# One PSUM bank per product and another order of operand sums in a two-layer network computed by seven-product matrix multiplication

## The chip, the cores and the metric

The kernel runs on one core of one Trainium2 chip. The metric is the device time of one execution in microseconds; the median of three executions of the kernel before is 1459.99 us (1458.37 to 1468.76).

## The reference, cut to what matters

```python
p_packed = sm_attn(p, k, v)                 # 8 x 8 heads, 576 tokens, 32 packed, 64 wide
x = sm_attn(q, p_packed, p_packed)          # put together: 4608 tokens x 512
h = max(max(x @ w1, x @ w2), x @ w3)        # 768 wide
x = h @ w_out                               # 512 wide
h = x @ w_in                                # 2048 wide    "third layer"
g = maximum(h, 0) + log1p(exp(-abs(h)))     # softplus
out = g @ w_out2                            # 512 wide     "fourth layer"
```

All arrays are 32-bit floats. The change concerns the last three lines alone.

## The kernel before, in words

The attention and the first two layers fill the first 508 us; they leave x in DRAM. What follows works on five blocks of tokens, numbered c = 0 to 4: three "wide" ones of 2 x 512 tokens and two "narrow" ones of 2 x 384 (`WIDE`, line 62). In each block the third layer runs first and the fourth after it.

**Precision.** Each fp32 operand is split into a high part (a ScalarE copy, line 126) and a low part (a VectorE subtraction, line 128), and each product of two tiles takes three matmuls (high x high, high x low, low x high).

**Seven products.** Both layers multiply in the Strassen-Winograd manner: a 2 x 2 partition of each operand, seven products of sums of the parts instead of eight products.

*Third layer* (`layer3`, line 1048, eight steps j per block). A step computes seven products, each a chain of six matmuls into one PSUM bank (`product`, line 1036). ScalarE copies the first product to SBUF (line 1061); VectorE adds the others to it in seven additions (`plus`, line 1059, each with one operand in PSUM and one in the SBUF tile `h`, which has one buffer); ScalarE then applies softplus to four results (line 1080) and writes them into the SBUF tiles `a00`, `a01`, `a10`, `a11` (in the code a11, a12, a21, a22). `bank` (line 1030) hands out the PSUM space: one tile of *two* banks for every *two* products, the first half to the one and the second half to the other; the pool has four such tiles (line 987), that is all eight banks. The framework puts in the waits between instructions that touch the same tile. Below, the product that gets the first half is called the even one, the other the odd one.

*Fourth layer* (`layer4`, line 1119). 28 steps v per block, four for each of seven products in the order P1, P5, P6, P2, P7, P3, P4 (line 65); a step takes twelve matmuls. `split_g(v)` (line 1104) makes the operand of step v in high and low parts, in tiles with three buffers; it is issued three steps ahead. Four products use sums of the parts of g: S1 = a21 + a22 (for P5), S3 = a11 - a21 (for P7), S2 = a22 - S3 (for P6), S4 = a12 - S2 (for P3). Before the change S1 is formed on VectorE inside `split_g` (line 1094), just ahead of the split that needs it; S3 on GpSimd during the first steps of the fourth layer (line 1102), S2 on VectorE after it, S4 on GpSimd in block 0 and on VectorE in the others. Results of products are added up in three chains X, Y, Z, each in a tile of two banks; `after` (line 1183) keeps a sum in SBUF, adds, transposes 32 x 32 blocks on VectorE (line 1150) and stores rows to DRAM through the SP queue (line 1174).

**What else sets the order.** The order of instructions on every engine is written out by hand: the program order is each engine's order (`manual_schedule`, line 1220). The lists `aside` (in the third layer) and `jobs` (after step v of the fourth) hold other work: in block 0 the splitting of both layers' weights (`split_weights`, line 1009), which come by `load_units` (line 995) into a pool of two buffers shared with x, and go back to DRAM in split form; in later blocks these are read back, 1792 KB for each step (`get_weights`, line 1022, a ring of three tiles). Also there: the sums and splits of the next block's x (`load_x2`, `sum_x2`, `split_x2`, four parts, three for a narrow block). All loads and stores of these stages go through the SP queue, in order.

Of the kernel before, what the change touches and what calls it, by code (L numbers as in the profile page):

```python
# [19 lines left out]
def packed_attention_maxout_softplus(  # L20
# [22 lines left out]
    nc = tc.nc  # L43
# [21 lines left out]
    PRODUCTS = ("P1", "P5", "P6", "P2", "P7", "P3", "P4")  # L65
# [710 lines left out]
    def narrow_wo(raw64, j, k):  # L776
# [29 lines left out]
        for o, in0, in1 in (  # L806
            (t[:, 0], a[:, 1], a[:, 0]),
            (t[:, 1], b[:, 1], t[:, 0]),
            (t[:, 2], b[:, 1], a[:, 1]),
            (t[:, 3], b[:, 0], t[:, 1]),  # L810
        ):
            nc.gpsimd.tensor_tensor(out=o, in0=in0, in1=in1, op=ALU.subtract)
        to_store.append((units(j, "P5", "P6"), t[:, 0:2]))
# [173 lines left out]
    psp = ctx.enter_context(tc.tile_pool(name="psp", bufs=4, space=PSUM, reuse_waits="tile"))  # L987
# [42 lines left out]
    def bank():  # L1030
        k = acc["products"] = acc.get("products", -1) + 1
        if k % 2 == 0:
            acc["bank"] = psp.tile([P, 2, CH], F32, tag="ps", name="ps_3")
        return acc["bank"][:, k % 2]

    def product(c, w, wi, xi):
        wide = BLOCKS[c][1]
        out = bank()[:, :wide]
# [9 lines left out]
    def layer3(c, j, aside):  # L1048
# [7 lines left out]
        h = cp.tile([P, 7, CH], F32, tag="h", name="h")[:, :, :wide]  # L1056
# [27 lines left out]
    def row(m, wide, i):  # L1084
        return m[:, i * 2 * CH : i * 2 * CH + 2 * wide].rearrange("p (b t) -> p b t", b=2)

    def sum_g(c, name, u, n=2):

        wide = BLOCKS[c][1]
        us = slice(u, u + n)  # L1090
        a11, a12, a21, a22 = (g[i, k][:, us, :wide] for i in range(2) for k in range(2))
        if name == "S1":
            t = row(mid[c], wide, 1 + u // 2 % 2)
            add(out=t, in0=a21, in1=a22, op=ALU.add)  # L1094
            return t
        out, in0, in1 = {"S3": (a21, a11, a21), "S2": (a11, a22, a21), "S4": (a11, a12, a11)}[name]
        return out, in0, in1

    def difference(c, name, v, engine):
        for u in (2 * v, 2 * v + 1) if engine is nc.gpsimd else (2 * v,):  # L1100
            out, in0, in1 = sum_g(c, name, u, 1 if engine is nc.gpsimd else 2)
            engine.tensor_tensor(out=out, in0=in0, in1=in1, op=ALU.subtract)  # L1102

    def split_g(c, v):
        pos, u = v // NU, 2 * (v % NU)
        wide = BLOCKS[c][1]
        key = {"P1": (0, 0), "P6": (0, 0), "P3": (0, 0), "P2": (0, 1), "P7": (1, 0), "P4": (1, 1)}
        if PRODUCTS[pos] == "P5":
            src = sum_g(c, "S1", u)
        else:  # L1110
            src = g[key[PRODUCTS[pos]]][:, u : u + 2, :wide]
# [7 lines left out]
    def layer4(c, v):  # L1119
# [4 lines left out]
        if first and v % NU == 0:  # L1124
            acc[CHAIN[name]] = psp.tile([P, 2, CH], F32, tag="ps", name="ps_4")
        ps = acc[CHAIN[name]]
        todo = []
        for i in range(2):
            u = 2 * (v % NU) + i
            tile_no, at = divmod(pos * FP + u, 7)  # L1130
            w = pairs[STEP * c + FP + tile_no]
            for b in range(2):
                for wl, x in ((0, ghi), (1, ghi), (0, glo)):
                    todo.append((i, b, u, w[:, wl, at, b], x[:, i], wl == 0 and x is ghi, x is glo))
        if c == NCH - 1 and v == NV - 1:
            todo.sort(key=lambda m: m[1])
        for i, b, u, l, r, head, tail in todo:
            nc.tensor.matmul(  # L1138
                ps[:, b, :wide],
# [4 lines left out]
                skip_group_check=name in ("P6", "P7", "P4", "P3"),  # L1144
            )

    def turn(c, half, h, src, b):

        o = outs[c, half]
        nc.vector.transpose(  # L1150
            out=o[:, :, h, b],
            in_=src[:, b].rearrange("p (r t) -> p r t", t=32),
        )

    def out_tile(c, half):

        tag = ("a01", "a10")[half]
        wide = BLOCKS[c][1]
        t = ap.tile([P, FP, CH], F32, tag=tag, name="o")
# [23 lines left out]
    def after(c, name):  # L1183

        wide = BLOCKS[c][1]
        m1, m5, u2 = (row(mid[c], wide, i) for i in range(3))
        ps = acc[CHAIN[name]][:, :, :wide]
        last = c == NCH - 1

        def result(m, half, h):  # L1190
            add(out=m, in0=m, in1=ps, op=ALU.add)
            for b in range(2):
                turn(c, half, h, m, b)

        if name in ("P1", "P5", "P6"):
            nc.scalar.activation(
                out={"P1": m1, "P5": m5, "P6": u2}[name], in_=ps, func=AF.Copy
            )
        elif name == "P2":
            out_tile(c, 0)  # L1200
            result(m1, 0, 0)
        elif name == "P7":
            out_tile(c, 1)
            result(m5, 1, 1)
            if last:
                store(c, 1, (1,), [nc.sync])
        elif name == "P3":
            result(u2, 0, 1)
            store(c, 0, (0, 1), [nc.sync])
        else:  # L1210
            for b in range(2):
                turn(c, 1, 0, ps, b)
            if last:
                store(c, 1, (0,), [nc.sync, nc.scalar])
            else:
                store(c, 1, (0, 1), [nc.sync])
# [3 lines left out]
    with tc.manual_schedule(engines={E.PE, E.DVE, E.Activation, E.Pool, E.SP}):  # L1220
        for c in range(NCH):
            more = parts[c + 1]
            for j in range(FP):
                aside = {0: [], 1: [], 2: [], 3: []}
                if c == 0:
# [4 lines left out]
                    aside[3].append((load_weights, j + 4))  # L1230
# [91 lines left out]
```

## Time and profile before

| | us |
|---|---|
| median of three executions | 1459.99 |
| the profiled execution, whole | 1461.07 |
| its span, first to last instruction | 1459.3 |
| TensorE busy within the span | 1268.3 |
| VectorE busy | 864.8 |
| ScalarE busy | 526.9 |
| GpSimd busy | 288.1 |

PE is TensorE's matmuls, DVE is VectorE, ACT ScalarE, POOL GpSimd, SPq the queue that issues DMAs. In a row of the trace, out<-in are the names of tiles in the program; the number in brackets at the end of a row is the idle time of the engine just before, and behind the arrow stands what ended it. PEclk is TensorE's granted clock as a share of full speed. Neighbouring matmuls overlap in the trace, so a matmul's price is read from the distance of starts and not from its duration.

### The profile page before, as it was taken

The page shows a single profiled execution, that of the slowest core. Times are in us where ns is not written, and L with a number is a line of the kernel's source. Part 1 is how long each engine was busy: PE and PEld are TensorE (multiplying, and loading weights), DVE is VectorE, ACT ScalarE, POOL GpSimd, SP SyncE. Part 2 cuts the span into 40 slices and gives each one's busy share as a digit, 9 for nine tenths or more (in the row PEclk, how much of TensorE's full clock was granted, in tenths as well). Part 3 has the DMA queues.
Part 4 walks back from the last instruction along what each step waited for, and adds up shares of the span by engine and source line. Part 5 has one row for each costly group of instructions (what it writes and reads, how often), then busy time and mean ns, then how long its engine had stood idle before and what let it go on. Part 6 is the DMA issues. An engine that isn't in the chain of part 4 may idle for free.

```text
span 1459.3 us, 21380 instructions
## 1 busy us (share of the span) xinstructions
PE 1268.3 (87%) x8599; PEld 1059.8 (73%) x8599; DVE 864.8 (59%) x1151; ACT 526.9 (36%) x767; POOL 288.1 (20%) x248
## 2 busy tenths in 40 slices
PE   8999999999999977777787779977789877897788
PEld 6788998898989955555565556755568766796678
DVE  3866665675765754578633459633387444853375
ACT  4734434344343433345312234312244222422242
POOL 2413122242331132035400015000050000400020
PEclk9999999999999999998899999999999999999999
DMA  9967768697672445446494335564345654575454
GB/s 249 282 170 196 184 179 230 168 242 209 195 203 78 163 187 188 169 140 212 147 311 154 117 113 215 166 223 152 105 161 192 234 197 170 186 251 203 175 197 149
DMA packets 117283, 272.25 MB, mean 187 GB/s; under 512 B 14785, under 2 KB 90305, under 8 KB 106945
## 3 DMA queue, kind: packets, MB, share of 16 engines
q1 hardware_dynamic: 111776, 261.26, 56.8%
q10 hardware_dynamic: 5408, 9.64, 1.8%
q8 instruction: 67, 1.10, 0.3%
q14 instruction: 32, 0.25, 0.1%
HBM read 211.09 MB, written 59.77 MB: 186 GB/s over the span
## 4 chain that ended last, share of the span: by engine, by line
PE 66%; DVE 17%; DMA 7%; issue 4%; ACT 4%; SPq 1%; POOL 1%; DVEq 0%; ACTq 0%; POOLq 0%
PE ps L482 23%; PE ps L1045 23%; PE ps L1138 15%; DVE h L1059 8%; DVE glo L128 3%; PE ps_w L460 2%; DVE a L1102 2%; DMA qraw<-in_q_dram 2%; DVE mid L1094 2%; DMA vt<-in_v_dram 2%; DMA xu<-x2d 1%; ACT ghi L126 1%; ACT a L1080 1%; DVE x2lo L128 1%; DVE wc L128 1%
## 5 line engine op out<-in xcount | busy, mean ns | idle before, releaser
L1045 PE MATMUL ps<-x2hi,wc 128*128 128x512 f32 (+1 forms) x1120 | 363.7, 385 | 127.0 <-DVE h L1059 106.2
L1059 DVE TENSOR_TENSOR h<-h,ps 128x512 f32<-128x512 f32 (+1 forms) x280 | 176.7, 634 | 306.7 <-PE ps L1045 305.3
L1045 PEld LDWEIGHTS ps<-x2hi,wc 128*128 128x128 f32 x1120 | 209.1, 189 | 205.6 <-DVE h L1059 151.9
L1138 PE MATMUL ps<-ghi,wc 128*128 128x512 f32 (+1 forms) x1120 | 340.9, 387 | 20.0 <-ACT ghi L126 20.0
L1138 PEld LDWEIGHTS ps<-ghi,wc 128*128 128x128 f32 x1120 | 216.3, 197 | 58.0 <-ACT ghi L126 26.6
L1138 PE MATMUL ps<-glo,wc 128*128 128x512 f32 (+1 forms) x560 | 219.3, 392 | 25.7 <-DVE glo L128 25.5
L1080 ACT ACTIVATE a<-h 128x512 f32<-128x512 f32 (+1 forms) x160 | 89.7, 584 | 370.9 <-DVE h L1059 370.8
L1102 POOL TENSOR_TENSOR a<-a,a 128x512 f32<-128x512 f32 (+1 forms) x48 | 79.7, 1685 | 684.7 <-DVE mid L1094 684.7
L1045 PE MATMUL ps<-x2lo,wc 128*128 128x512 f32 (+1 forms) x560 | 207.8, 371 | 0.0
L128 DVE TENSOR_TENSOR glo<-a,ghi 128x1024 fp32r<-128x1024 f32 (+1 forms) x120 | 143.0, 1204 | 46.7 <-ACT ghi L126 46.2
L126 ACT ACTIVATE ghi<-a 128x1024 fp32r<-128x1024 f32 (+1 forms) x120 | 115.2, 970 | 118.6 <-PE ps L1138 90.4
L1138 PEld LDWEIGHTS ps<-glo,wc 128*128 128x128 f32 x560 | 109.4, 195 | 54.4 <-DVE glo L128 38.8
L482 PE MATMUL ps<-a2hi,pwhi 128*128 128x288 f32 x576 | 127.6, 303 | 0.1
L482 PE MATMUL ps<-a2hi,pwlo 128*128 128x288 f32 x576 | 123.2, 296 | 0.4 <-DVE pwlo L128 0.4
L482 PE MATMUL ps<-a2lo,pwhi 128*128 128x288 f32 x576 | 123.2, 295 | 0.2 <-DVE a2lo L128 0.2
L1045 PEld LDWEIGHTS ps<-x2lo,wc 128*128 128x128 f32 x560 | 105.9, 189 | 10.9
L128 POOL TENSOR_TENSOR hlo<-m,hhi 128x576 fp32r<-128x576 f32 x41 | 59.2, 1443 | 238.8 <-ACT hhi L126 232.9
L482 PEld LDWEIGHTS ps<-a2hi,pwhi 128*128 128x128 f32 x576 | 91.6, 189 | 15.0 <-ACT m L509 5.3
L511 DVE TENSOR_TENSOR m<-ps,m 128x576 f32<-128x576 f32 x96 | 72.4, 754 | 49.0 <-PE ps L482 47.0
L482 PEld LDWEIGHTS ps<-a2hi,pwlo 128*128 128x128 f32 x576 | 92.6, 188 | 0.6 <-DVE pwlo L128 0.6
L482 PEld LDWEIGHTS ps<-a2lo,pwhi 128*128 128x128 f32 x576 | 92.5, 188 | 0.4 <-DVE a2lo L128 0.4
L128 DVE TENSOR_TENSOR pwlo<-ps_w,pwhi 128x1024 fp32r<-128x1024 f32 (+1 forms) x40 | 44.5, 1113 | 78.3 <-ACT pwhi L126 78.3
(106 smaller groups left out, 1563.9 us busy)
## 6 DMA issues: line engine op xcount, KB each, us to landing
wc<-wic SPq DMA_DIRECT2D x32, 1792.0 KB
wc<-woc SPq DMA_DIRECT2D x32, 1792.0 KB
qraw<-in_q_dram SPq DMA_DIRECT2D x112, 140.0 KB
wic<-wc SPq DMA_DIRECT2D x8, 1792.0 KB
woc<-wc SPq DMA_DIRECT2D x8, 1792.0 KB
kraw<-in_k_dram SPq DMA_DIRECT2D x96, 140.0 KB
vt<-in_v_dram SPq DMA_DIRECT2D x8, 1152.0 KB
wraw<-in_moe_w_dram SPq DMA_DIRECT2D x18, 512.0 KB
```

The source lines that it names most:

```text
L126: nc.scalar.activation(out=hi, in_=src, func=AF.Copy)
L128: engine.tensor_tensor(out=lo, in0=src, in1=hi.bitcast(F32), op=ALU.subtract)
L460: nc.tensor.matmul(ps[cols, G, : units * P].rearrange("p (w x) -> p w x", w=units), ppT[n][rows, cols], wsb[rows, 4 * c : 4 * c + units, g ...
L482: nc.tensor.matmul(o, w, xx, start=first, stop=last)
L511: nc.vector.tensor_tensor(out=m, in0=ps[:, :, :HS], in1=ms[n, f], op=ALU.max)
L1045: nc.tensor.matmul(out, l, r, start=(i == 0), stop=(i == len(terms) - 1))
L1059: add(out=h[:, o], in0=h[:, a], in1=ps, op=ALU.add)
L1080: nc.scalar.activation(out=g[half, k][:, j, :wide], in_=h[:, 2 * k + half], func=AF.Softplus)
L1094: add(out=t, in0=a21, in1=a22, op=ALU.add)
L1102: engine.tensor_tensor(out=out, in0=in0, in1=in1, op=ALU.subtract)
L1138: nc.tensor.matmul(ps[:, b, :wide], l, r, start=first and u == 0 and head, stop=u == FP - 1 and tail, skip_group_check=name in ("P6", "P7" ...
```

## The change

Every product of the third layer, and each half of a chain of the fourth, gets a PSUM tile of one bank; the pool has eight of these. The order of the fourth layer's products becomes P1, P2, P6, P5, P7, P3, P4. S3 is formed during the third layer: on GpSimd after each step in blocks 1 to 4; on VectorE, in pairs, within the steps in block 0. S2, S1 and S4 are formed on VectorE after steps 0 to 3, 4 to 7 and 8 to 11, in all blocks; S2 gets room of its own in a larger `mid` tile, S1 = a11 + S2 and S4 = a12 - S2 are formed in place. `sum_x2` moves from GpSimd to VectorE within the fourth layer, and from VectorE to GpSimd within the third; the x parts of blocks 1 to 4 are split at steps 12, 14, 18 and 22 instead of 0, 2, 9 and 17. The matmuls within a step go operand by operand with both banks, instead of bank by bank. Results are added and transposed bank by bank.

```diff
-    PRODUCTS = ("P1", "P5", "P6", "P2", "P7", "P3", "P4")
+    PRODUCTS = ("P1", "P2", "P6", "P5", "P7", "P3", "P4")
...
-    psp = ctx.enter_context(tc.tile_pool(name="psp", bufs=4, space=PSUM, reuse_waits="tile"))
+    psp = ctx.enter_context(tc.tile_pool(name="psp", bufs=8, space=PSUM, reuse_waits="tile"))
...
-    def bank():
-        k = acc["products"] = acc.get("products", -1) + 1
-        if k % 2 == 0:
-            acc["bank"] = psp.tile([P, 2, CH], F32, tag="ps", name="ps_3")
-        return acc["bank"][:, k % 2]
+    def bank(name):
+        return psp.tile([P, CH], F32, tag="ps", name=name)
...
-        h = cp.tile([P, 7, CH], F32, tag="h", name="h")[:, :, :wide]
+        h = cp.tile([P, 10, CH], F32, tag="h", name="h")[:, :, :wide]
...
+    def form(c, name, u, n, engine):
+        us = slice(u, u + n)
+        a11, a12, a21, a22 = (
+            g[i, k][:, us, : BLOCKS[c][1]] for i in range(2) for k in range(2)
+        )
+        s2 = None if name == "S3" else row(c, 1 + u // 2)
+        out, in0, in1, op = {
+            "S3": (a21, a11, a21, ALU.subtract),
+            "S2": (s2, a22, a21, ALU.subtract),
+            "S1": (a11, a11, s2, ALU.add),
+            "S4": (a12, a12, s2, ALU.subtract),
+        }[name]
+        engine.tensor_tensor(out=out, in0=in0, in1=in1, op=op)
...
-            acc[CHAIN[name]] = psp.tile([P, 2, CH], F32, tag="ps", name="ps_4")
+            acc[CHAIN[name]] = [bank("ps_4") for b in range(2)]
...
-            for b in range(2):
-                for wl, x in ((0, ghi), (1, ghi), (0, glo)):
+            for wl, x in ((0, ghi), (1, ghi), (0, glo)):
+                for b in range(2):
...
+                    if j and j % 2 == 0:
+                        aside[1].append((form, c, "S3", j - 2, 2, nc.vector))
...
-                            aside[1].append((sum_x2, c + 1, part))
+                            aside[1].append((sum_x2, c + 1, part, nc.gpsimd))
...
+                if c:
+                    form(c, "S3", j, 1, nc.gpsimd)
...
+                jobs[0].append((form, c, "S3", FP - 2, 2, nc.vector))
...
-                for part in range(more):
-                    v = 3 + 4 * part
+                for part, v in enumerate((7, 12, 16, 21)):
+                    jobs[v - 1].append((sum_x2, c + 1, part))
+                    jobs[v].append((split_x2, c + 1, part))
...
-                for part, v in zip(range(more), (0, 2, 9, 17)):
+                for part, v in zip(range(more), (12, 14, 18, 22)):
...
             for i in range(NU):
-                jobs.setdefault(1 + i, []).append((difference, c, "S3", i, nc.gpsimd))
-                jobs.setdefault(3 + i, []).append((difference, c, "S2", i, nc.vector))
-                jobs.setdefault(11 + i, []).append(
-                    (difference, c, "S4", i, nc.gpsimd if c == 0 else nc.vector)
-                )
+                for name, v in (("S2", 0), ("S1", 4), ("S4", 8)):
+                    jobs[v + i].append((form, c, name, 2 * i, 2, nc.vector))
+            done = {
+                3: [(keep_sum, c, "X", 0)],
+                11: [(keep_sum, c, "X", 1)],
+                13: [(out_tile, c, 0), (result, c, 0, 0, "Z", 0)],
+                15: [(keep_sum, c, "Y", 2)],
+                19: [(out_tile, c, 1), (result, c, 1, 1, "X", 2)],
+                23: [(result, c, 0, 1, "Y", 1), (store, c, 0, (0, 1), [nc.sync])],
+                27: [(result, c, 1, 0, "X")],
+            }
```

## Rows read from the trace of the kernel before

**Rows 1.** The page's first part: busy time of TensorE and the other engines.

```profile
PE 1268.3 (87%) x8599; PEld 1059.8 (73%) x8599; DVE 864.8 (59%) x1151; ACT 526.9 (36%) x767; POOL 288.1 (20%) x248
```

**Rows 2.** Windows: third and fourth layer of blocks 0, 1, 3, 4 in turn.

```profile
core 0: us, PE busy (x) PEld busy (x) DVE busy (x) ACT busy (x) POOL busy (x), PEclk, DMA share, GB/s
508.28:624.26 115.98, 85.11 (x339) 61.19 (x337) 56.20 (x73) 39.98 (x58) 21.31 (x24) 1.00 0.53 195
624.26:743.10 118.84, 92.82 (x337) 69.97 (x336) 85.91 (x64) 47.69 (x51) 51.66 (x32) 0.87 0.54 177
743.10:855.11 112.01, 85.77 (x338) 61.83 (x336) 44.00 (x67) 24.72 (x40) 0.00 (x0) 0.99 0.46 165
855.11:944.47 89.36, 83.87 (x338) 64.45 (x337) 69.29 (x56) 37.80 (x39) 27.33 (x16) 0.96 0.49 167
...
1145.41:1233.89 88.48, 66.22 (x338) 57.27 (x336) 35.88 (x67) 20.25 (x40) 0.00 (x0) 1.00 0.57 207
1233.89:1303.00 69.11, 63.24 (x338) 59.95 (x337) 52.21 (x54) 29.54 (x37) 16.30 (x12) 0.98 0.59 208
1303.00:1390.59 87.59, 66.22 (x338) 57.27 (x337) 32.90 (x59) 20.25 (x40) 0.00 (x0) 1.00 0.53 197
1390.59:1453.71 63.12, 60.01 (x337) 58.00 (x336) 44.25 (x48) 24.72 (x31) 10.78 (x8) 1.00 0.56 193
```

**Rows 3.** The page's groups: matmuls of the third layer, idle time before them.

```profile
L1045 PE MATMUL ps<-x2hi,wc 128*128 128x512 f32 (+1 forms) x1120 | 363.7, 385 | 127.0 <-DVE h L1059 106.2
```

**Rows 4.** Timeline, third layer of block 2: start, duration, instruction.

```profile
958.08 0.50 PE L1045 MATMUL ps<-x2hi,wc 128*128 128x512 f32 x1 [0.78 <-DVE h L1059]
958.42 0.39 PE L1045 MATMUL ps<-x2lo,wc 128*128 128x512 f32 x1
...
959.35 0.62 PE L1045 MATMUL ps<-x2hi,wc 128*128 128x512 f32 x2
...
959.84 0.60 ACT L1061 ACTIVATE h<-ps 128x512 f32<-128x512 f32 x1 [0.62 <-PE ps L1045]
...
961.19 0.69 DVE L1059 TENSOR_TENSOR h<-h,ps 128x512 f32<-128x512 f32 x1 [3.17 <-PE ps L1045]
...
961.93 0.50 PE L1045 MATMUL ps<-x2hi,wc 128*128 128x512 f32 x1 [0.84 <-DVE h L1059]
```

**Rows 5.** Timeline of ScalarE, fourth layer, a wide and a narrow block.

```profile
930.38 1.06 ACT L126 ACTIVATE ghi<-a 128x1024 fp32r<-128x1024 f32 x1 [1.75 <-PE ps L1138]
...
1288.18 0.85 ACT L126 ACTIVATE ghi<-a 128x768 fp32r<-128x768 f32 x1 [1.27 <-PE ps L1138]
```

**Rows 6.** Groups by form, VectorE: count | busy us, mean ns | idle before.

```profile
L128 DVE TENSOR_TENSOR glo<-a,ghi 128x1024 fp32r<-128x1024 f32 x15 | 18.1, 1214 | 7.4 <-ACT ghi L126 7.4
L1150 DVE STREAM_TRANSPOSE o<-mid 128x512 f32<-128x512 f32 x6 | 3.9, 690 | 0.1
...
L884 DVE TENSOR_TENSOR xu<-xu 128x256 f32<-128x256 f32 x8 | 3.0, 421 | 0.1
...
L1102 DVE TENSOR_TENSOR a<-a,a 128x1024 f32<-128x1024 f32 x4 | 8.1, 2024 | 0.0
```

**Rows 7.** Timeline, third layer of block 0: GpSimd beside VectorE.

```profile
527.79 3.79 POOL L884 TENSOR_TENSOR wu<-wu 128x256 f32<-128x256 f32 x4 [7.46 <-DMA wu<-wi]
528.06 1.55 DVE L128 TENSOR_TENSOR wc<-wu,wc 128x1024 fp32r<-128x1024 f32 x1
529.53 0.67 DVE L1059 TENSOR_TENSOR h<-h,ps 128x512 f32<-128x512 f32 x1
```

**Rows 8.** Timeline, fourth layer of block 0: a weight load and its reader.

```profile
674.49 0.43 SPq L998 DMA_DIRECT2D wu<-wof  x1
...
683.96 1.06 ACT L126 ACTIVATE wc<-wu 128x1024 fp32r<-128x1024 f32 x1 [6.01 <-DMA wu<-wof]
```

**Rows 9.** DMA issues, and one window (columns as in rows 2).

```profile
wc<-wic SPq DMA_DIRECT2D x32, 1792.0 KB
...
1300.00:1320.00 20.00, 16.13 (x85) 14.21 (x85) 6.59 (x12) 3.50 (x7) 0.00 (x0) 1.00 0.99 340
```

More of the change, by code (lines that the diff above doesn't have):

```diff
@@ L1028, in get_weights @@
             )
[L1030 to L1034 removed]
+    def bank(name):
+        return psp.tile([P, CH], F32, tag="ps", name=name)
     def product(c, w, wi, xi):
         wide = BLOCKS[c][1]
[L1038 removed]
+        out = bank("ps_3")[:, :wide]
         terms = [
@@ L1143, in layer4 @@
                 stop=u == FP - 1 and tail,
-                skip_group_check=name in ("P6", "P7", "P4", "P3"),
+                skip_group_check=not first,
             )
[L1147 to L1152, printed above, removed]
-        )
     def out_tile(c, half):
-        tag = ("a01", "a10")[half]
         wide = BLOCKS[c][1]
-        t = ap.tile([P, FP, CH], F32, tag=tag, name="o")
+        t = ap.tile([P, FP, CH], F32, tag=("a00", "a10")[half], name="o")
         outs[c, half] = t.rearrange("p j t -> p (j t)")[:, : 4 * wide].rearrange(
@@ L1181, in store, with result, keep_sum @@
             r += count
-    def after(c, name):
+    def result(c, half, h, chain, m=None):
         wide = BLOCKS[c][1]
[L1186 to L1195, printed above, removed]
+        for b in range(2):
+            src = acc[chain][b][:, :wide]
+            if m is not None:
+                kept = row(c, m)[:, b]
+                add(out=kept, in0=kept, in1=src, op=ALU.add)
+                src = kept
+            nc.vector.transpose(
+                out=outs[c, half][:, :, h, b], in_=src.rearrange("p (r t) -> p r t", t=32)
+            )
+    def keep_sum(c, chain, m):
+        for b in range(2):
             nc.scalar.activation(
-                out={"P1": m1, "P5": m5, "P6": u2}[name], in_=ps, func=AF.Copy
+                out=row(c, m)[:, b], in_=acc[chain][b][:, : BLOCKS[c][1]], func=AF.Copy
             )
[L1199 to L1216, printed above, removed]
     E = mybir.EngineType
@@ L1221, in packed_attention_maxout_softplus @@
         for c in range(NCH):
-            more = parts[c + 1]
+            more, last = parts[c + 1], c == NCH - 1
             for j in range(FP):
@@ new lines, in packed_attention_maxout_softplus @@
+            done = {
[7 more added lines that the diff above has]
+            }
+            if last:
+                done[19].append((store, c, 1, (1,), [nc.sync]))
+                done[27].append((store, c, 1, (0,), [nc.sync, nc.scalar]))
+            else:
+                done[27].append((store, c, 1, (0, 1), [nc.sync]))
@@ L1277, in packed_attention_maxout_softplus @@
                     split_g(c, v + 3)
-                if v % NU == NU - 1:
-                    after(c, PRODUCTS[v // NU])
-                for fn, *args in jobs.get(v, ()):
+                for fn, *args in done.get(v, []) + jobs[v]:
                     fn(*args)
```

69 lines of the change are left out of this document (26 added, 43 removed).

## The prediction, made before the changed kernel was run

> **What bounds the kernel now.** I read the busy times first: TensorE is busy 1268 of 1459 us [rows 1], so the question is where it is not, and where its busy time is slower than it need be. Windows cut at the first matmul of each layer of each block answer that [rows 2]. All of the first 508 us lie ahead of the change. Of the rest, a third layer takes 116.0, 112.0, 112.0 (block 2 is like block 1), 88.5 and 87.6 us, a fourth layer 118.8, 89.4, 89, 69.1 and 63.1 us, though both hold 336 matmuls of the same shape. So the third layer loses time everywhere and the fourth mostly in block 0.
>
> The undisturbed price is read in the fourth layer, where ScalarE makes one operand per step and then waits for TensorE to finish a step: 1.06 + 1.75 = 2.81 us for twelve matmuls in a wide block, 0.85 + 1.27 = 2.12 us in a narrow one [rows 5]. So 28 steps cost 78.7 and 59.4 us, and so should a third layer of the same 336 matmuls.
>
> In the third layer the groups show 127.0 us of idle time ahead of matmuls, nearly all ended by VectorE's additions [rows 3]. The timeline shows the pattern [rows 4]: the row at 959.35 holds two matmuls, the last of one product and the first of the next (even) one, which starts without a wait, in a fresh tile, while ScalarE's copy of the one before only begins at 959.84; but the odd product at 961.93 starts 0.05 us after the addition that read the even one's result ended (961.19 + 0.69), after 0.84 us of idling. It writes the other half of the same tile. So in 280 products 140 wait for a read of the other bank of their tile, 127.0/140 = 0.91 us each, and then lose 0.11 us more, as the step behind a restart is 0.34 us (958.08 to 958.42) and not 0.23 (2.81/12).
>
> **The change part by part.** *One bank per product.* Neighbouring products share no tile, so the wait for the reader of the product before goes; what is left is the wait for the reader of the eighth product before. What is late next? VectorE and ScalarE need per step, one behind the other at worst: seven additions of 0.69, the copy of 0.60 [rows 4] and two softplus behind the last addition (0.6 each, an estimate from the copy of the same shape), with hand-over about 6.8 us, against 42 x 2.81/12 = 9.84 us on TensorE; a narrow step has about three quarters of both (an estimate). TensorE stays the bound, 8 x 9.84 = 78.7 and 59.4 us per layer. The price of a wait that stays is bounded by today's 112.0 and 88.5.
>
> *S3 on GpSimd in the third layer, blocks 1 to 4.* One operation a step, nothing else of weight there. It slows VectorE only where that reads SBUF alone: beside GpSimd a split took 1.55 us, the addition with a PSUM operand 0.67 as ever [rows 7]. Cost 0; if the cover were gone, eight operations a block. The same holds for two `sum_x2` there.
>
> *Block 0's third layer.* Beside the seven additions VectorE has two splits of weights (1.2 to 1.55 and about 0.95) and in three of eight steps an S3 of 1.21: 6.8 + 2.5 + 1.2 = 10.5 us at worst in those, 9.3 in the others, around 9.84. The eight banks even this out: 81 us. Ends: 78.7, and 116.0 if nothing is gained.
>
> One rule is weighed here. The Trainium skill, "SBUF — State Buffer", section "Who interferes with whom", says that a VectorE instruction with two SBUF inputs and a GpSimd one that reads SBUF exclude each other for a whole instruction. The rows show 0.34 us lost (1.55 against 1.21), less than one of the four GpSimd operations (3.79/4 = 0.95). By the rule two or three VectorE instructions a step would lose up to 0.95 each, some 1.5 us more in six steps, and the total below would be 9 us higher.
>
> *Fourth layer, blocks 1 to 4.* It loses 10.7, 10, 9.7 and 3.7 us now (89.4 - 78.7 and so on). S1 was formed right ahead of the split that needed it, beside GpSimd, where an operation of VectorE took 2.02 us instead of 1.21 [rows 6]. After the change GpSimd is idle there and S2, S1, S4 come several steps ahead of need. VectorE per step: split 1.21 + sum 1.21 = 2.4 of 2.81 in steps 0 to 11; steps 12 to 14 with two x parts (2 x (1.21 + 0.91, three quarters of it as an estimate)) and one result (1.21 + 2 x 0.69 = 2.6) 3 x 1.21 + 4.2 + 2.6 = 10.4 against 8.4, within the two steps of lead that a split has; later groups are alike. A narrow block has three quarters of all but the x parts: 8.9 against 6.4 in steps 12 to 14, still within the lead of about 3 us. I take 1 us a layer: 79.7 and 60.4. Ends: 78.7, and today's 89.4.
>
> *Fourth layer, block 0: 118.8 us, 40.1 over the 78.7.* Of these about 15 are the lower clock (0.87 [rows 2]: TensorE falls to 1.2 GHz in places after long waits), the rest waits. Two things remain. First, VectorE's work: 28 splits and 13 sums of 1.21, 12 splits of weights (6 x 2.12), 8 of x (4 x 2.12), 16 additions of x (0.42 each, now here instead of on GpSimd), three results (2.6) and the last transposes (1.4) are 49.6 + 12.7 + 8.5 + 6.7 + 7.8 + 1.4 = 87 us, more than the 78.7 of TensorE. Second, the weights: a load is issued when the split of the tile two before is done, takes 9.5 us from issue to its reader (674.49 to 683.96 [rows 8]; a 1792 KB store stands ahead of it in the same queue), and ScalarE reaches that reader three or four steps (8.4 or 11.2 us) later, minus some 3 us that the last split took. Where it is three it stands about 6 us, with all operands queued behind it. I walked the 28 steps with these prices: TensorE is on time to step 10, loses 1.5 us by step 14, 7.4 at step 15 (a late weight tile, then x's sums and S4 ahead of the operand on VectorE), 4 by step 20, 4.5 at step 22 (the last weight tile) and 3 more: 100 us, and 3 for the clock after the two long waits: 103. Ends: VectorE without any wait, 87 less what stands beside TensorE's tail, so 85; and today's 118.8.
>
> *Bank by bank at the end.* The last block's transposes can start on the first bank while the second is summed: the 5.6 us after the last matmul (1459.3 - 1453.71) become 5.
>
> *SP's queue.* Stores of results now read the tile `a00` instead of `a01`, which the next block's first softplus writes; the store is issued four steps ahead of the block's end: no cost, 2 us a boundary at the outside. Weight loads of 1792 KB per step come every 9.84 or 7.4 us instead of 13.4 or 11. A window with 340 GB/s was reached [rows 9], 5.4 us per load: hidden, with the rival below as the other end.
>
> *Sum.* Start 508.3; block 0: 81 + 103; blocks 1 and 2: 2 x (78.7 + 79.7); blocks 3 and 4: 59.4 + 60.4 and 59.4 + 59.4; end 5: 508.3 + 184 + 316.8 + 238.6 + 5 = 1252.7 us of span. The profiled execution took 1.8 us more than its span (1461.07 against 1459.3) and stood 1.1 us above the median of the runs shown: 1252.7 + 1.8 - 1.1 = **1253 us**.
>
> **The rivals.** *A: transfers become the bound.* A narrow block moves 16 x 1.835 MB of weights and about 3.1 MB of x and results (768 tokens x 512 x 4 bytes each way): 32.5 MB, today in 157.6 us at 207 GB/s, then in 119 us at 273. If no more than 250 is sustained between stores of small rows, it takes 130 us: 11 us more for each of two narrow blocks, and the wide ones (33.6 MB in 158 us, 212 GB/s) hold. With block 0's fourth layer, which has the densest stores, back at 118.8: 1253 + 22 + 16 = 1291. For it: the queue is full (0.99) at a block's beginning. Against: in that window 340 GB/s flowed.
>
> *B: the wait stays.* If the reads hold up the odd product for another reason than the shared tile, the third layers keep 516.1 us instead of 357.2 and only the fourth layers gain: 1253 + 159 = 1412. Against: even products never wait.
>
> *C: slower.* If the wait is tied to the product just before whatever its bank, and the even one is spared today only because its tile is one whose readers are long done, then with a tile for each product all 280 are tied to it: 140 more waits of 0.91 + 0.11 us on top of B, 1412 + 143 = 1555. From about 47 additional waits on (48 us gained in the fourth layers / 1.02) the kernel is slower than before. Against: the even product at 959.35 ran while its neighbour's bank was still unread [rows 4]. The Trainium skill, "PSUM — Partial Sum Buffer", section "PSUM bank collisions raise a hardware error", has engines excluded from each other only within a bank; the trace agrees as far as that row goes.
>
> *D: better.* Block 0's loads come sooner, as the tighter order issues them sooner: its fourth layer at 85, its third at 79: 1233.
>
> **How the numbers follow.** The forecast 0.70, A 0.12, D 0.08, B 0.06, C 0.04. Range: from D's 1233 to A's 1291, opened to 1230 and 1292, which leaves out B and C. A measurement of this kernel tells about 1% (14.6 us) from no change; all cases but C are faster by more: faster 0.95, within 1% 0.01, slower 0.04.
>
> **What would show it.** Right: idle time ahead of line 1045's matmuls falls from 127 to under 15 us; third layers of 79 and 59 us; GpSimd all but idle in the fourth layers; the fourth layer of block 0 the only one with waits of several us, ended by weight loads and VectorE's splits. Wrong: third-layer steps above 10.5 us in blocks 1 to 4, ended by an addition (C or B) or by a load of weights (A).

## The result, and the profile after

The changed kernel takes 1243.65 us (median of four runs, 1240.78 to 1247.03) beside 1459.18 us for the kernel before on the same chip: a ratio of 0.8512 [0.8469, 0.8555]. The forecast was 1253 us, its range 1230 to 1292. The profiled execution took 1240.78 us with a span of 1239.0 us. In the kernel after, the third layer's matmuls stand in line 1042, its additions in 1056, the copy in 1058 and softplus in 1077; the fourth layer's matmuls in 1135, the operand sums in 1099.

The page's first part, against [rows 1]:

```profile
PE 1207.5 (97%) x8599; PEld 1062.0 (86%) x8599; DVE 831.5 (67%) x1182; ACT 526.8 (43%) x782; POOL 213.2 (17%) x224
```

As many matmuls as before now fill 97% of the span instead of 87%. TensorE's own busy time fell as well, by 61 us. Windows cut at the first matmul of each layer, third and fourth layer of blocks 0, 1, 3 and 4 in turn, with the columns of [rows 2]:

```profile
506.62:582.82 76.20, 76.20 (x338) 63.09 (x337) 55.29 (x74) 38.72 (x57) 20.25 (x24) 1.00 0.76 275
582.82:687.39 104.57, 87.47 (x337) 65.82 (x336) 82.15 (x92) 48.27 (x55) 0.00 (x0) 0.92 0.63 211
687.39:764.31 76.92, 76.45 (x338) 62.98 (x336) 38.40 (x57) 24.11 (x39) 14.68 (x15) 1.00 0.71 249
764.31:843.02 78.71, 78.71 (x337) 63.28 (x336) 66.16 (x71) 38.68 (x43) 1.29 (x1) 1.00 0.56 190
...
997.89:1056.16 58.27, 58.27 (x337) 58.26 (x336) 30.67 (x56) 19.75 (x39) 12.74 (x15) 1.00 0.85 315
1056.16:1115.52 59.36, 59.36 (x337) 59.36 (x337) 50.21 (x65) 30.07 (x41) 1.02 (x1) 1.00 0.69 242
1115.52:1174.31 58.79, 58.73 (x337) 58.15 (x337) 30.51 (x56) 19.74 (x39) 7.09 (x7) 1.00 0.79 293
1174.31:1233.83 59.52, 59.52 (x337) 59.20 (x336) 43.25 (x55) 25.38 (x35) 1.02 (x1) 1.00 0.60 205
```

In seven of the ten stages (block 2, not shown, has 76.16 and 78.71) length and PE busy are the same number: TensorE never stands still. In the third layers of blocks 1 and 4 it stands still for 0.47 and 0.06 us. The one stage with real gaps is block 0's fourth layer: 104.57 us long, 87.47 busy, at a granted clock of 0.92. The five third layers together fell from 516.2 to 346.3 us, the five fourth layers from 429.2 to 380.9.

The page's groups of matmuls, against [rows 3] (the number ahead of the arrow is the idle time):

```profile
L1042 PE MATMUL ps<-x2hi,wc 128*128 128x512 f32 (+1 forms) x1120 | 322.2, 367 | 0.5 <-DMA wc<-wic 0.5
L1135 PE MATMUL ps<-ghi,wc 128*128 128x512 f32 (+1 forms) x1120 | 287.7, 378 | 9.1 <-ACT ghi L126 9.0
```

The 127.0 us ahead of the third layer's matmuls became 0.5, and that rest belongs to a load, not to an addition. Timeline of the third layer of block 1, PE and DVE, against [rows 4]:

```profile
854.35 0.62 PE L1042 MATMUL ps<-x2hi,wc 128*128 128x512 f32 x2
854.81 0.39 PE L1042 MATMUL ps<-x2lo,wc 128*128 128x512 f32 x1
855.03 0.62 PE L1042 MATMUL ps<-x2hi,wc 128*128 128x512 f32 x2
...
855.61 0.69 DVE L1056 TENSOR_TENSOR h<-h,ps 128x512 f32<-128x512 f32 x1 [2.18 <-ACT h L1058]
```

Three matmuls take 855.03 - 854.35 = 0.68 us, 0.227 each, straight through the additions on VectorE; a step of 42 takes 9.52 us (76.20/8). What is left shows in the list of waits (who waited <- for whom: us in total, times, longest):

```profile
ACT wc L126 <- DMA wu<-wof: 30.0, 4, 10.0
DVE wc L128 <- ACT wc L126: 17.8, 4, 7.6
...
PE ps L1135 <- ACT ghi L126: 9.0, 2, 4.7
...
PE ps L1135 <- DVE glo L128: 7.9, 6, 2.0
```

All four rows belong to block 0's fourth layer. ScalarE stands 30.0 us for four late weight tiles; VectorE then stands for ScalarE; TensorE stands 17 us for the operands queued behind both.

### The profile page after: what moved, and what is told of

Read it like the earlier page. It is cut to its first block, busy times and chain, and to the rows that moved or that the text cites. A ratio compares the mean times of both kernels' runs of the same rounds, so it can differ in the third digit from the quotient of the medians.

```text
span 1239.0 us, 21402 instructions
## 1 busy us (share of the span) xinstructions
PE 1207.5 (97%) x8599; PEld 1062.0 (86%) x8599; DVE 831.5 (67%) x1182; ACT 526.8 (43%) x782; POOL 213.2 (17%) x224
## 4 chain that ended last, share of the span: by engine, by line
PE 87%; DMA 5%; DVE 4%; issue 2%; ACT 1%; SPq 1%; DVEq 0%; ACTq 0%
PE ps L482 31%; PE ps L1042 27%; PE ps L1135 24%; PE ps_w L460 2%; DMA wu<-wof 2%; PE ps_s L287 1%; DVE glo L128 1%; DMA wc<-wic 1%; DMA wraw<-in_moe_w_dram 1%; PE ps_v L358 1%; PE ps_e L331 1%; DMA xu<-x2d 1%; DVE wc L128 0%; DVE x2lo L128 0%; DMA praw<-in_p_dram 0%
## 5 line engine op out<-in xcount | busy, mean ns | idle before, releaser
L1042 PE MATMUL ps<-x2hi,wc 128*128 128x512 f32 (+1 forms) x1120 | 322.2, 367 | 0.5 <-DMA wc<-wic 0.5
L1135 PE MATMUL ps<-ghi,wc 128*128 128x512 f32 (+1 forms) x1120 | 287.7, 378 | 9.1 <-ACT ghi L126 9.0
L1056 DVE TENSOR_TENSOR h<-h,ps 128x512 f32<-128x512 f32 (+1 forms) x280 | 173.6, 633 | 155.5 <-PE ps L1042 116.1
L1135 PEld LDWEIGHTS ps<-ghi,wc 128*128 128x128 f32 x1120 | 209.5, 191 | 42.1 <-ACT ghi L126 10.8
L1135 PE MATMUL ps<-glo,wc 128*128 128x512 f32 (+1 forms) x560 | 168.3, 379 | 8.0 <-DVE glo L128 7.9
L128 DVE TENSOR_TENSOR glo<-a,ghi 128x1024 fp32r<-128x1024 f32 (+1 forms) x120 | 132.0, 1110 | 33.8 <-ACT ghi L126 33.2
L1099 POOL TENSOR_TENSOR a<-a,a 128x512 f32<-128x512 f32 (+1 forms) x32 | 36.8, 1151 | 567.3 <-ACT a L1077 567.3
L1135 PEld LDWEIGHTS ps<-glo,wc 128*128 128x128 f32 x560 | 104.4, 190 | 27.5 <-DVE glo L128 12.7
```

Source lines behind the costliest of these rows:

```text
L128: engine.tensor_tensor(out=lo, in0=src, in1=hi.bitcast(F32), op=ALU.subtract)
L1042: nc.tensor.matmul(out, l, r, start=(i == 0), stop=(i == len(terms) - 1))
L1056: add(out=h[:, o], in0=h[:, a], in1=ps, op=ALU.add)
L1099: engine.tensor_tensor(out=out, in0=in0, in1=in1, op=op)
L1135: nc.tensor.matmul(ps[b][:, :wide], l, r, start=first and u == 0 and head, stop=u == FP - 1 and tail, skip_group_check=not first,)
```

## The experiments

Twelve runs were made, ten edited kernels and two repeats, in three groups that each shared the runs of the kernel before (1463.25, 1461.80 and 1463.32 us).

### Which part gives what

**E1, the banks alone.** The kernel before, with only its PSUM tiles changed (and, as these ask for it, the fourth layer's results copied and added bank by bank); sums, product order and jobs stay as before.

```diff
-    psp = ctx.enter_context(tc.tile_pool(name="psp", bufs=4, space=PSUM, reuse_waits="tile"))
+    psp = ctx.enter_context(tc.tile_pool(name="psp", bufs=8, space=PSUM, reuse_waits="tile"))
...
+    def bank(name):
+        return psp.tile([P, CH], F32, tag="ps", name=name)
...
-            acc[CHAIN[name]] = psp.tile([P, 2, CH], F32, tag="ps", name="ps_4")
+            acc[CHAIN[name]] = [bank("ps_4") for b in range(2)]
```

> The kernel before with one change: every product and each half of a chain gets a tile of one bank, eight tiles; sums, their order and their engines as before. Theory (an odd product waited for the reader of the other half of its tile): the third layers fall from 516 to about 346 us, as in the changed kernel; the fourth layers stay near their 429 us; time 1285 to 1305 us. Rival 1 (the waits went because S3 and the x sums moved, not because of the banks): third layers stay near 516 us, time 1440 to 1460. Rival 2 (the two parts need each other): fourth layers grow by tens of us as sums come later against a faster TensorE, time above 1330.

Measured: 1296.13 us (1292.7 to 1302.58), ratio 0.8862 [0.8823, 0.8901]. Its third layers take 76.20, 76.18, 76.17, 58.27 and 59.40 us, so the banks alone are the whole gain there. Its fourth layers take 434.9 us together, 5.7 more than before. The window of E1's fourth layer of block 0, and its two largest waits of matmuls:

```profile
581.57:701.69 120.12, 92.13 (x338) 68.58 (x336) 88.73 (x71) 48.36 (x55) 50.62 (x32) 0.89 0.56 188
```

```profile
PE ps L1135 <- DVE glo L128: 28.2, 28, 6.9
...
PE ps L1135 <- ACT ghi L126: 22.1, 16, 2.8
```

GpSimd works 50.62 us in that stage, and over the five blocks TensorE waits for operands 44 times: the fourth layer as it was.

**E2, everything but the banks.** The kernel after, with a tile of two banks for two neighbouring products again, and one of two banks for each chain.

```diff
-    psp = ctx.enter_context(tc.tile_pool(name="psp", bufs=8, space=PSUM, reuse_waits="tile"))
+    psp = ctx.enter_context(tc.tile_pool(name="psp", bufs=4, space=PSUM, reuse_waits="tile"))
...
+    def bank():
+        k = acc["products"] = acc.get("products", -1) + 1
+        if k % 2 == 0:
+            acc["bank"] = psp.tile([P, 2, CH], F32, tag="ps", name="ps_3")
+        return acc["bank"][:, k % 2]
```

> The changed kernel with tiles of two banks again, two products to a tile, as before; order of products and sums as changed. Theory: third layers back at about 516 us, with 0.9 us of idle time ahead of 140 odd products; fourth layers keep 105 + 2 x 79 + 59 + 60 = 381 us; time 1405 to 1420. Rival (the sums pay only beside the banks): fourth layers at 429 us again, time about 1455.

Measured: 1411.35 us (1410.59 to 1412.22), ratio 0.9646 [0.9612, 0.968]. Third layers 513.5 us together, fourth layers 380.0. Windows of E2, third and fourth layer of block 1, and its waits:

```profile
729.65:840.10 110.45, 84.85 (x337) 61.03 (x336) 41.22 (x59) 24.73 (x40) 14.59 (x15) 1.00 0.49 173
840.10:920.14 80.04, 80.04 (x337) 64.28 (x336) 64.13 (x67) 38.28 (x42) 1.28 (x1) 0.98 0.55 187
```

```profile
PE ps L1045 <- DVE h L1059: 104.6, 120, 3.9
...
PE ps L1045 <- ACT h L1061: 20.8, 20, 1.2
```

120 + 20 = 140 waits: one for each odd product, as in the kernel before. E1 gains 167.1 us, E2 51.9; together 219.0, and the full change gained 1461.80 - 1242.92 = 218.9 in the second group of runs. The two parts add up: neither needs the other.

**E4, two banks per tile, but not of neighbours.** E2, with products k and k + 4 in one tile; its pool of four tiles is the same.

```diff
-        if k % 2 == 0:
-            acc["bank"] = psp.tile([P, 2, CH], F32, tag="ps", name="ps_3")
-        return acc["bank"][:, k % 2]
+        if k % 8 < 4:
+            acc["bank", k % 4] = psp.tile([P, 2, CH], F32, tag="ps", name="ps_3")
+        return acc["bank", k % 4][:, k // 4 % 2]
```

> As the second kernel, with tiles of two banks, but products k and k+4 share a tile instead of neighbours. Theory (the wait is for the reader of the other half, which here is long done): third layers 346 us, 1240 to 1255 us. Rival (a tile of two banks costs a wait whoever shares it): third layers near 516 us, 1405 to 1420.

Measured: 1241.1 us in a single execution, as fast as the full change; third layers 76.2, 77.1, 76.2, 58.3 and 58.4 us. The group of its third-layer matmuls:

```profile
L1045 PE MATMUL ps<-x2hi,wc 128*128 128x512 f32 (+1 forms) x1120 | 322.1, 367 | 0.4 <-DMA wc<-wic 0.4
```

So neither the size of a tile nor the number of tiles made the wait, but which two products share one. A matmul that starts a bank waits for readers of the tile's other bank, whose addition is due just then for the neighbour and long done for the product four before. The framework's wait goes by the tile. (The Trainium skill, "PSUM — Partial Sum Buffer", section "PSUM bank collisions raise a hardware error", keeps engines apart by bank. The trace agrees: the wait in E2 went beyond that, and in E1 and the kernel after, where the neighbour's bank is a tile of its own, matmuls run on while it is read, with 0.5 us of idle time in the rows of the kernel after.)

**E3, how many banks it takes.** The kernel after, with two of the eight banks for the third layer and six for the fourth.

```diff
-        return psp.tile([P, CH], F32, tag="ps", name=name)
+        return psp.tile([P, CH], F32, tag=name, name=name, bufs=2 if name == "ps_3" else 6)
```

> The changed kernel with only two one-bank tiles for the third layer's products (the other six for the fourth layer's chains). Theory (it is the sharing with the neighbour that cost, not the number of banks): a product waits for the reader of the product two before, which ends 0.75 us after that one, while the next takes 1.36 us; no wait in most places, some in block 0 where splits stand between the additions: 1241 to 1265 us. Rival (TensorE needs the run ahead of eight banks): one wait per product or step comes back, third layers 80 to 160 us longer in sum, 1320 to 1400.

Measured: 1298.86 us (1294.71 to 1302.23), ratio 0.8874 [0.884, 0.8908]. That is a miss: third layers 400.9 us, 55 more than with eight banks. Its wait, and the timeline at one of these waits:

```profile
PE ps L1042 <- DVE h L1056: 31.3, 40, 1.5
```

```profile
886.58 1.41 DVE L1056 TENSOR_TENSOR h<-h,ps 128x512 f32<-128x512 f32 x2 [0.67 <-PE ps L1042]
...
887.32 0.50 PE L1042 MATMUL ps<-x2hi,wc 128*128 128x512 f32 x1 [0.78 <-DVE h L1056]
```

40 waits in 40 steps: one per step, at its sixth product; a middle step of a wide block takes 10.79 us instead of 9.52. The fourth product is read by two additions that lie apart in the program. The row at 886.58 holds the addition of the fifth product (0.7 us) and then the second reading of the fourth; the sixth product starts at 887.32, when the first of these is over and the second still runs. The fourth product holds one bank for all that time, and one bank alone is left for its successors. The expected 1241 to 1265 us left out how long one result is held.

**E8, two banks and the fourth product copied out.** E3, with a ScalarE copy of that product to SBUF, which both additions then read.

```diff
-        ps = product(c, w, 3, 3)
+        ps = h[:, 7]
+        nc.scalar.activation(out=ps, in_=product(c, w, 3, 3), func=AF.Copy)
```

> The kernel with two banks for the third layer; the fourth product of a step, which two additions read, is first copied to SBUF by ScalarE, so its bank is free at once. If the one wait per step came from that product holding a bank until the fifth one's addition: third layers from 401 back to 346 to 355 us, time 1240 to 1255. If two banks are too few anyway: 1285 to 1300.

Measured: 1265.44 us in a single execution, between the two theories; third layers 369.0 us. Its waits:

```profile
PE ps L1042 <- DVE h L1056: 6.2, 10, 1.1
```

In blocks 1 to 4 a middle step falls from 10.79 to 9.71 us (wide) and from 8.57 to 7.63 us (narrow): the long hold was the cause of most of it there. Block 0's steps stay at 9.7 to 11.4 us, with the splits of weights between the additions, and the first two steps of a block wait up to 3 us more. That rest was not taken apart. Eight banks cover all of it.

### The fourth layer in blocks 1 to 4

**E10, sums just ahead of need.** The kernel after, with S2 and S1 of blocks 1 to 4 formed inside `split_g`, just ahead of the split that needs them. S4 stays early.

```diff
+        if c and name in ("P6", "P5"):
+            form(c, {"P6": "S2", "P5": "S1"}[name], 2 * i, 2, nc.vector)
...
-                    jobs[v + i].append((form, c, name, 2 * i, 2, nc.vector))
+                    if c == 0 or name == "S4":
+                        jobs[v + i].append((form, c, name, 2 * i, 2, nc.vector))
```

> The changed kernel with S2 and S1 of blocks 1 to 4 formed on VectorE right ahead of the split that needs them, as S1 was before the change, but with GpSimd idle and the new order of products. If the lead of several steps is what the sums' 48 us came from: VectorE forms (1.2), waits for the copy (1.06), subtracts (1.2), 3.5 us a step against 2.81 in eight steps, 2 to 6 us a block after the lead of the splits is used up: 1251 to 1267. If it was the crowding (x parts and GpSimd in the same steps): no more than 1 us a block, 1241 to 1247.

Measured: 1273.29 us (1272.9 to 1273.6), ratio 0.8711 [0.8689, 0.8732]. The fourth layers of blocks 1 to 4 take 86.6, 86.6, 67.4 and 65.5 us: of the 34.1 us that the full change gained in these four layers (310.4 to 276.3) 29.8 are gone, with no operation added and GpSimd all but idle (1.3 us a layer). Timeline of E10, VectorE and ScalarE, in block 1, first two steps with S2, then two with S1:

```profile
784.69 1.23 DVE L128 TENSOR_TENSOR glo<-mid,ghi 128x1024 fp32r<-128x1024 f32 x1 [1.21 <-ACT ghi L126]
...
788.26 1.23 DVE L128 TENSOR_TENSOR glo<-mid,ghi 128x1024 fp32r<-128x1024 f32 x1 [1.21 <-ACT ghi L126]
...
801.24 2.35 DVE L1099 TENSOR_TENSOR a<-a,mid 128x1024 f32<-128x1024 f32 x2
...
803.71 1.06 ACT L126 ACTIVATE ghi<-a 128x1024 fp32r<-128x1024 f32 x1 [3.64 <-DVE a L1099]
...
804.80 1.23 DVE L128 TENSOR_TENSOR glo<-a,ghi 128x1024 fp32r<-128x1024 f32 x1 [1.20 <-ACT ghi L126]
...
805.94 2.35 DVE L1099 TENSOR_TENSOR a<-a,mid 128x1024 f32<-128x1024 f32 x2
```

A ring has closed: two sums (2.35), ScalarE's copy (1.06), its subtraction on VectorE (1.23), next two sums: 805.94 - 801.24 = 4.70 us per step, where TensorE needs 2.81. It is so for the operands of steps 12 to 14, where S4 and S1 meet in VectorE's queue, and TensorE takes 4.70 us for each of these steps. Where S2 stands alone ahead of its split the ring takes 788.26 - 784.69 = 3.57 us, and TensorE still keeps 2.81 in steps 8 to 10, as the splits are three steps ahead; but each such step uses up 0.76 us of that lead. So a late sum has a price, hidden at first, and a second sum in the same queue makes it larger. The expectation had the ring of one sum (3.5 us) and the lead; it did not count S4 in the same queue, and so came out at 1251 to 1267 us. In the kernel after, TensorE has no idle time in these layers (78.71 us long, 78.71 busy).

What the run does not show is that the lead alone would be enough: the change also emptied GpSimd and moved the x parts, and E10 keeps both.

**E7, S3 later in the program.** The eight parts of S3 of blocks 1 to 4 stand behind the third layer in the program, not within it.

```diff
-                if c:
-                    form(c, "S3", j, 1, nc.gpsimd)
...
+            if c:
+                for j in range(FP):
+                    form(c, "S3", j, 1, nc.gpsimd)
```

> The changed kernel with S3 in blocks 1 to 4 formed on GpSimd at the beginning of the fourth layer instead of during the third. Theory (the gain of the sums lies in forming them steps ahead of need, by the new order of products, and the third layer as the place is worth little): the S2 sums follow S3 at 3.5 us apiece on GpSimd, are done near step 6 and are needed at step 8; 0 to 3 us a block: 1243 to 1256. Rival (the place of S3 carries most of the 48 us that the sums were worth): 8 to 12 us a block, 1272 to 1292.

Measured: 1243.66 us (1242.35 to 1245.65), ratio 0.8507 [0.8492, 0.8523]: as the full change. But the edit did not move the work. Windows of E7, third and fourth layer of block 1 (GpSimd is POOL, the fifth pair of numbers):

```profile
691.50:768.42 76.92, 76.45 (x337) 62.98 (x336) 38.29 (x57) 24.08 (x39) 14.64 (x15) 1.00 0.70 249
768.42:847.14 78.72, 78.72 (x338) 63.28 (x336) 66.14 (x71) 38.68 (x43) 1.30 (x1) 1.00 0.54 188
```

GpSimd works 14.64 us in the third layer and 1.30 in the fourth; in the kernel after it is 14.68 and 1.29. GpSimd's queue has no other work left at that point, so each part of S3 starts when softplus has written its operands, wherever its line stands. E7 is in effect the full change once more: what the place of S3 is worth was not tested.

### The fourth layer of block 0

The full change ran again in the group of the next kernels. 

> The changed kernel once more, as the measure for the three beside it: 1240 to 1247 us.

Measured: 1242.92 us (1242.75 to 1244.75), ratio 0.8506 [0.8491, 0.8521]; block 0's fourth layer 104.4 us.

**E5, the load ahead of the store.** The store of a split weight tile, with which `split_weights` ended, becomes a job of its own behind the load of the next tile.

```diff
-            nc.sync.dma_start(
-                out=(wic[s] if s < FP else woc[s - FP]),
-                in_=t.rearrange("p h a k x -> p (h a k x)").bitcast(F32),
-            )
...
+    def store_weights(s):
+        nc.sync.dma_start(
+            out=(wic[s] if s < FP else woc[s - FP]),
+            in_=pairs[s].rearrange("p h a k x -> p (h a k x)").bitcast(F32),
+        )
...
+                    aside[3].append((store_weights, j + 2))
+                    jobs[v + 1].append((store_weights, FP + t + 2))
```

> The changed kernel with one exchange in block 0: the load of the next weight tile is issued ahead of the store of the one just split, not behind it. Theory (in block 0's fourth layer ScalarE stands still because each load of 896 KB queues behind a store of 1792 KB): the 9.5 us from issue to reader become about 5, ScalarE's waits for these loads fall from 30 us to 10 to 15, the layer from 104.6 to 92 to 97 us; time 1230 to 1237. Rival (VectorE's 87 us of work set that layer, or the loads are slow by themselves): 102 to 105 us, time 1239 to 1247.

Measured: 1231.98 us (1229.04 to 1233.2), ratio 0.8423 [0.8407, 0.844]. SP's issues and ScalarE's reader of the same tile, in the kernel after, with the window from the load's issue to its reader:

```profile
623.06 0.33 SPq L1017 DMA_DIRECT2D woc<-wc  x1
623.43 0.43 SPq L998 DMA_DIRECT2D wu<-wof  x1
...
632.54 1.06 ACT L126 ACTIVATE wc<-wu 128x1024 fp32r<-128x1024 f32 x1 [9.37 <-DMA wu<-wof]
```

```profile
623.43:632.54 9.11, 6.81 (x28) 4.84 (x27) 4.14 (x4) 0.00 (x1) 0.00 (x0) 1.00 0.87 302
```

And in E5, with the same window, that of the whole layer, and its wait:

```profile
623.35 0.36 SPq L998 DMA_DIRECT2D wu<-wof  x1
623.75 0.56 SPq L1019 DMA_DIRECT2D woc<-wc  x1
...
629.70 1.06 ACT L126 ACTIVATE wc<-wu 128x1024 fp32r<-128x1024 f32 x1 [6.86 <-DMA wu<-wof]
```

```profile
623.35:629.70 6.35, 6.29 (x27) 4.79 (x26) 4.51 (x4) 0.00 (x1) 0.00 (x0) 1.00 0.71 228
584.52:678.79 94.27, 83.81 (x338) 63.16 (x336) 82.03 (x92) 48.34 (x55) 0.00 (x0) 0.98 0.68 236
```

```profile
ACT wc L126 <- DMA wu<-wof: 15.0, 4, 6.9
```

From issue to reader it is 6.4 us (629.70 - 623.35) instead of 9.1 (632.54 - 623.43), and ScalarE was there before the tile both times. In the kernel after the DMA engines are busy for 0.87 of that stretch, and at 302 GB/s 2.75 MB pass in it: the store (1.84 MB) and the load (0.92 MB) together. The four loads with a wait took 10.0, 9.1, 9.4 and 10.4 us, and in E5 6.7, 6.4, 6.0 and 5.9. The four waits halve to 15.0 us, the layer shrinks by 10.3, and the granted clock rises from 0.92 to 0.98 with the shorter waits, which is part of that (PE busy 87.47 to 83.81). This kernel is faster than the kernel before and than the full change (1242.75 to 1244.75 us in the same group).

**E5 again**, in the third group of runs. 

> The kernel with the load ahead of the store once more, beside the next ones: 1229 to 1234 us.

Measured: 1233.15 us (1229.89 to 1241.01), ratio 0.844 [0.8413, 0.8467]; the layer takes 94.3 us.

**E6, less work for VectorE.** The kernel after, with block 0's sums of x in the fourth layer on GpSimd, as before the change.

```diff
-                    jobs[v - 1].append((sum_x2, c + 1, part))
+                    jobs[v - 1].append((sum_x2, c + 1, part, nc.gpsimd))
```

> The changed kernel with block 0's four sums of x in the fourth layer on GpSimd, as before the change. If VectorE's amount of work sets that layer, 6.7 us less of it give 97 to 99 us there and 1234 to 1238. If the late weight loads set it, the layer stays within 3 us of 104.6 (VectorE's operations beside GpSimd take up to 2.0 us instead of 1.2, which takes back what the move gives): 1240 to 1250.

Measured: 1244.63 us (1243.79 to 1249.47), ratio 0.852 [0.85, 0.8539]; the layer takes 106.4 us. VectorE is busy for 81.83 us of it, against 82.15 in the kernel after: the move hardly relieved it, for the reason that E9 shows. So this run does not tell whether relief for VectorE would help.

**E9, both edits.** E5 and E6 together.

> Load ahead of the store, and block 0's sums of x on GpSimd in the fourth layer. If with the loads early VectorE's amount of work is the bound, 6.7 us less of it bring the layer from 94.3 to 88 to 90 us: 1225 to 1229. If the operations that VectorE runs beside GpSimd take back what the move gives, as without the exchange: 94 to 97 us, 1231 to 1236.

Measured: 1235.73 us (1231.97 to 1236.65), ratio 0.8449 [0.8428, 0.8469]; the layer takes 94.7 us. The groups by form, in that layer alone, first of E5:

```profile
L128 DVE TENSOR_TENSOR glo<-a,ghi 128x1024 fp32r<-128x1024 f32 x24 | 28.7, 1213 | 2.2 <-ACT ghi L126 2.2
...
L884 DVE TENSOR_TENSOR xu<-xu 128x256 f32<-128x256 f32 x16 | 6.1, 420 | 2.2 <-DMA xu<-x2d 2.0
```

and of E9:

```profile
L128 DVE TENSOR_TENSOR glo<-a,ghi 128x1024 fp32r<-128x1024 f32 x24 | 30.3, 1283 | 2.2 <-ACT ghi L126 2.2
...
L884 POOL TENSOR_TENSOR xu<-xu 128x256 f32<-128x256 f32 x16 | 24.2, 1534 | 88.5 <-DVE glo L128 52.4 <-DMA xu<-x2d 35.8
```

The sixteen sums cost VectorE 6.1 us (16 x 0.42 = 6.7 without overlap) and GpSimd 24.2; beside them VectorE's other operations get longer (24 splits by 1.6 us), so that its busy time falls by 82.03 - 80.85 = 1.2 us only. Most of GpSimd's time is waiting, as the first of its sums in E9 shows, with ScalarE's reader:

```profile
610.35 5.97 POOL L884 TENSOR_TENSOR xu<-xu 128x256 f32<-128x256 f32 x1 [52.42 <-DVE glo L128]
...
616.36 1.06 ACT L126 ACTIVATE x2hi<-xu 128x1024 fp32r<-128x1024 f32 x1 [5.93 <-POOL xu L884]
```

The shortest of the sixteen takes 0.74 us; this one lasts as long as five VectorE operations on SBUF tiles that follow each other without a gap (610.23 to 615.73). ScalarE waits for the slow sums, 16.9 us in this layer against 7.2 for VectorE's in E5. What keeps this layer at 94 and not at 78.7 us was not separated further: VectorE is busy 82 of the 94, and neither E6 nor E9 took enough work from it to tell.

## Why the prediction was right

**The mechanism held.** The shared tile made the odd product wait (E2, E4), the banks removed it with nothing in its place (E1), and in blocks 1 to 4 the sums set ahead of need gave most of the rest (E10). Rival B was priced at 1412 us as the case in which only the fourth layers gain; E2, which is that case, took 1411.35. Rival C fell with E1 and E4: no product became tied to the one before it. Of D the faster third layer of block 0 came, the faster fourth did not.

**By its steps**, in us of span (first numbers predicted, then found): start 508.3, 506.6; block 0 81 and 103, 76.2 and 104.6; blocks 1 and 2 each 78.7 and 79.7, found 76.9 and 78.7, then 76.2 and 78.7; block 3 59.4 and 60.4, 58.3 and 59.4; block 4 59.4 and 59.4, 58.8 and 59.5; end 5, 5.1. The span is 13.7 us shorter than predicted (terms rounded): 10.9 in the third layers, 1.7 at the start, 1.3 in the fourth layers, and the end 0.1 the other way. The start is scatter: it lies between 505.4 and 510.7 us in the runs here. Against the median it is 9.4, as the profiled run lies 2.9 us below that and had been taken 1.1 above.

**The term that was mis-sized is the third layer's pace.** It was taken over from the fourth, 2.81/12 = 0.234 us for a matmul, 9.84 for a step. Found were 0.227 and 9.52 (narrow: 7.28 for 7.42). The trace before held that pace too. Matmuls of block 2's third layer, beside those of [rows 4]:

```profile
960.03 0.61 PE L1045 MATMUL ps<-x2hi,wc 128*128 128x512 f32 x2
...
960.71 0.39 PE L1045 MATMUL ps<-x2hi,wc 128*128 128x512 f32 x1
```

From 959.35 to 960.03 and on to 960.71 three matmuls take 0.68 us each time, 0.227 apiece. Why the same shape runs 3% faster in the one layer than in the other, both at a granted clock of 1.00, stays open. The second size was the wait's: 0.91 + 0.11 us. Block 1 fell from 112.01 to 76.92, which is 1.25 us for each of 28 waits: 26.2 us were idle (112.01 - 85.77), 0.94 each, and 9.3 us lay in TensorE's busy time (85.77 to 76.45). The trace shows where: the last matmul ahead of the stop at 961.93 starts at 960.71 and counts as busy for 0.39 us, though in a running stream it costs 0.227. So 0.16 us of every stop are booked as busy, which the sum left out; 0.11 are the step behind the restart, and the rest of the 1.25 the slightly longer steps after it.

**Block 0's third layer** was given 2.3 us for an uneven load on VectorE. None came: eight banks bridge it, and each step takes 9.5 us. The Trainium skill, "SBUF — State Buffer", section "Who interferes with whom", has a VectorE instruction with two SBUF inputs and a GpSimd one that reads SBUF keep each other out; by that, the sum was to be 9 us higher. GpSimd's additions of that layer in the trace after (shortest, median and longest in ns):

```profile
L884 POOL TENSOR_TENSOR wu<-wu x24: 730/739/1517, 508.0 to 555.6; 128x256 f32<-128x256 f32 x24
```

The trace agrees that each waits for the other: three 128x768 splits that found an addition under way took 1.18 to 1.33 us, the others 0.95, and additions that found a split under way took up to 1.52 us instead of 0.74. The prediction had looked at VectorE's side alone. The estimate of 9 us was too large, as one VectorE operation a step met GpSimd, lost 0.38 us at most, and the layer lost nothing.

**Block 0's fourth layer** came out at 104.6 against 103, with long waits where the walk had put them: steps 14 and 15 take 7.26 and 7.63 us, steps 21 and 22 take 7.69 and 5.29 (walked: 15 and 22). That the total fits so well is in part luck. The walked losses add up to 20.4 us, which makes 99.1 and not 100; found were 5.2 by step 13 (walked 1.5 by 14), 9.3 in 14 and 15 (7.4), 4.0 to step 20 (4), 7.4 in 21 and 22 (4.5) and 0.1 after (3). And 3 us were given to the clock, where TensorE's busy time lies 8.8 us above the undisturbed 78.7 at a granted clock of 0.92 (87.47), while it idled 17.1. E5 confirms the store ahead of the load as the cause of 10.3 us. The walk put the loss on loads and VectorE's work alike; VectorE's share stays open, as E6 and E9 did not relieve it.

**Fourth layers of blocks 1 to 4** lose nothing; the 1 us given to three of them did not come. The cost of S3 in the third layer was put at nothing, and so it is: block 2's third layer takes 76.16 us with it and 76.17 without (E1). That it gains something by standing there no run shows (E7).

**Rival A** is excluded. The narrow third layers, where it would decide, move 315 and 293 GB/s where it took 250 for the most that is sustained, and the idle time ahead of line 1042 that loads ended is 0.5 us in all.

## What to carry to other kernels

Two results that follow each other in time should not share a tile whose waits are set for the whole tile: place in one tile what is written and read far apart, and count banks by how long each result is held, not by how many are being written. Form operand sums steps ahead of need, and look above all at places where two of them stand in one queue ahead of the same operand. Read in the trace when an operation ran before judging its place: a line moved within an otherwise empty queue moves nothing. When a load that someone will wait for and a store that nobody waits for go into one queue together, issue the load first.

## What the runs showed of the hardware that was not expected

A store of 1792 KB issued 0.4 us ahead of a load in the same queue delayed the reader by 2.7 us (9.1 against 6.4 from issue to reader); the DMA engines, busy for 0.63 of that layer on average, were busy for 0.87 of that stretch. The same 128x512 matmuls had a steady distance of 0.227 us in the third layer and 0.234 in the fourth, at a granted clock of 1.00 each time. A stop of TensorE in block 1 of the kernel before cost 1.25 us on average, where the trace shows 0.94 of idle time. And one GpSimd addition of 0.74 us lasted 5.97 beside five VectorE operations in a row.
